# Scores of 28 tiles as two 64-row matmuls into two PSUM banks, in an attention and max-FFN kernel

## The chip, the cores and the metric

The kernel runs on one core of one Trainium2 chip. The metric is device microseconds of one execution. Nothing runs on the other cores.

## The reference, cut to what matters

Two parts follow each other. The first is attention over 8 batches and 8 heads (head size 64) with 512 local and 32 global positions. A local query sees the 32 global keys and the local keys at most 32 positions away; a global query sees everything. The second is a feed-forward over the 4352 resulting rows of 512: three products, their maximum, and a product back.

```python
s_ll = scale * np.matmul(q_l, k_l.transpose(0, 1, 3, 2))
mask = np.abs(pos[:, None] - pos[None, :]) <= window          # window = 32
s_l = np.concatenate([scale * np.matmul(q_l, k_g.transpose(0, 1, 3, 2)), np.where(mask, s_ll, -1e9)], axis=-1)
out_l = np.matmul(sm(s_l), np.concatenate([v_g, v_l], axis=2))
...
h = np.maximum(np.maximum(x @ w1, x @ w2), x @ w3)            # 512 -> 768
return (h @ w_out).astype(np.float32)                          # 768 -> 512
```

Only the scores `q k^T` of the local queries are touched by the change; the numbers that come out are the same.

## The kernel before, in words

**Tiles.** A tile is 128 query positions of a pair of heads (j = 0 and 1). Each of the 32 pairs (4 pairs per batch) has four tiles t = 0 to 3, so there are 128 tiles; t = 0 and 3 have 192 keys, t = 1 and 2 have 224 (`WIN`). One turn of the main loop (line 567) treats tile i, and calls in this order: `trans` of tile i+1 (its probabilities are turned by TensorE, lines 362 and 363), some matmuls of the feed-forward of the batch before (`fill`, lines 441 and 462), `scores` of tile i+3 (lines 335 or 339), more feed-forward, `pv` of tile i (probabilities times values, lines 401 or 409), and the work on weights and loads. The first 16 tiles go in an order of their own (`SEQ`), with tile halves of the keys (`kh`). `glob` (lines 285 and 289) makes the scores of the global queries, `late` (lines 504, 513, 519) those of the first batch, which were left out at the start.

**Split and unsplit.** Most products are made of operands that were split into a high and a low part and go through TensorE as `F32R`. For the first tiles the split would cost VectorE, ScalarE and GpSimd time that they need for the weights, so the scores of tiles 0 to 27 (`NATK`) and the products with values of tiles 0 to 25 (`NAT`) take plain `F32` operands. These are the unsplit tiles. A plain matmul shows in the trace as two passes, each with a weight load of its own.

**The scores of an unsplit tile.** The key tile holds the 64 dimensions of head 0 on partitions 0 to 63 and those of head 1 on partitions 64 to 127. The stationary operand is 128x128 for each head: the host writes head 0's queries over 64 rows of zeros, and for head 1 zeros over the queries (`qz`, lines 643 to 647). Each matmul thus takes all 128 rows, and both heads' results lie in one PSUM bank, `ps[:, 0:224]` and `ps[:, 224:448]`.

**What follows a score.** VectorE takes mask, scale and row minimum in one instruction per head (line 342), ScalarE the exponential (line 344), then come the sum's reciprocal and the multiplication (lines 347, 348 and the helper `times`, lines 121, 123, 125).

**PSUM.** `pm` has three banks for the feed-forward. `psS` has two one-bank buffers (name `S` in the trace): scores, the turned global probabilities (line 381), the global scores and those of `late`. `psT` has one bank (`T`). `psO` has one buffer of two banks (`O`): `pv` and the last product of `late`. `pv` copies its result out into `xr` (helper `copy`, lines 113 and 115).

**Weights.** The 24 weight blocks arrive in double precision and are taken apart by ScalarE (line 175), VectorE (176, 177, 180, 181) and a split (103, 113, 115), one or two blocks per tile (`WS`).

**Order.** Helpers choose an engine by a running cost sum (`least`). Within that the tile framework places every instruction on its engine by a planned time and adds the semaphores; the order of the source is not the order of the engines, and where an instruction may start decides where it is put. DMAs go out on SP's queue in its order.

Of the kernel before, what the change touches and what calls it, by code (L numbers as in the profile page):

```python
# [9 lines left out]
F32 = mybir.dt.float32  # L10
# [8 lines left out]
B, H, SL, SG, D = 8, 8, 512, 32, 64  # L19
DM, DF = 512, 768  # L20
NP = H // 2
# [4 lines left out]
NATK = range(0, 28)  # L26
# [24 lines left out]
def f32(ap):  # L51
    return ap.bitcast(F32)


def body(ctx, tc, kin, qin, vin, min_, win, out):
    nc = tc.nc
    act, dve, pool, pe = nc.scalar, nc.vector, nc.gpsimd, nc.tensor

    const = ctx.enter_context(tc.tile_pool(name="const", bufs=1))
    att = ctx.enter_context(tc.tile_pool(name="att", bufs=2))  # L60
# [3 lines left out]
    psS = ctx.enter_context(tc.tile_pool(name="psS", bufs=2, space=PSUM))  # L64
    psT = ctx.enter_context(tc.tile_pool(name="psT", bufs=1, space=PSUM))
    psO = ctx.enter_context(tc.tile_pool(name="psO", bufs=1, space=PSUM))
# [15 lines left out]
    def spend(es, ns):  # L82
        for e in es:
            load[e] += ns
# [122 lines left out]
    NAT = 26  # L207
    EARLY = 16
    SEQ = [4 * p + t for h in range(2) for p in range(NP) for t in (2 * h, 2 * h + 1)] + list(range(16, NS))
    kraw, kst, qraw, qs, vraw, vs, xr, sc, pg, pts = [{} for _ in range(10)]  # L210
# [32 lines left out]
    def load_q(s):  # L243
        if s < NS:
            if s in NATK:
                e = s < EARLY and SEQ.index(s) % 2
                qraw[s] = att.tile([128, 256], F32, name="qn", tag="qraw" if e else "qs")
            else:
                qraw[s] = att.tile([128, 256], F32, name="qraw")
            nc.sync.dma_start(out=qraw[s], in_=qin[s])  # L250

    def split_q(s):
        if s < NS and s not in NATK:
# [60 lines left out]
    def scores(sl):  # L314
        if sl >= NS:
            return
        p, t = divmod(sl, 4)
        c0, n = WIN[t]
        ps = psS.tile([128, 512], F32, name="S")
        if sl < EARLY:  # L320
            s = sc[sl] = early[:, SEQ.index(sl) % 4]
        else:
            s = att.tile([128, 2, 224], F32, name="s")
            sc[sl] = prob[sl % 2]
        nm = small.tile([128, 2], F32, name="nm")
        z = small.tile([128, 2], F32, name="z")
        ph = [ps[:, 0:224], ps[:, 224:448]]
        if sl < EARLY:
            keys, c0 = khalf[p][0], c0 - khalf[p][1]
        elif sl in NATK:  # L330
            keys = kraw[p]
        for j in range(2):
            if sl in NATK:

                pe.matmul(ph[j][:, 0:n], lhsT=qraw[sl][:, 128 * j:128 * j + 128], rhs=keys[:, c0:c0 + n],  # L335
                          start=True, stop=True)
                continue
            for a in range(2):
                pe.matmul(ph[j][:, 0:n], lhsT=qs[sl][:, a, 128 * j:128 * j + 128],  # L339
                          rhs=kst[p][:, j, c0:c0 + n], start=(a == 0), stop=(a == 1))  # L340
        for j in range(2):
            dve.tensor_tensor_reduce(out=s[:, j, 0:n], in0=ph[j][:, 0:n], in1=mask[:, (1, 0, 1, 0)[t], 32 * (t == 0):32 * (t == 0) + n],  # L342
                                     scale=-0.125, scalar=3.0e38, op0=ALU.add, op1=ALU.min, accum_out=nm[:, j:j + 1])
            act.activation(out=s[:, j, 0:n], in_=s[:, j, 0:n], func=AF.Exp, bias=nm[:, j:j + 1], scale=-1.0,  # L344
                           accum_out=z[:, j:j + 1])
        for j in range(2):
            dve.tensor_scalar(out=z[:, j:j + 1], in0=z[:, j:j + 1], scalar1=1e-9, scalar2=None, op0=ALU.add)  # L347
            dve.reciprocal(out=z[:, j:j + 1], in_=z[:, j:j + 1])
            times(s[:, j, 0:n], s[:, j, 0:n], z[:, j:j + 1])
        if sl >= EARLY:  # L350
            nc.sync.dma_start(out=f32(sc[sl])[:, :, 0:n], in_=s[:, :, 0:n])
        spend("d", 2 * (n * 1.04 + 75) + 150)
        spend("a", 2 * (n * 0.833 + 278))
# [37 lines left out]
    def pv(sl):  # L391
        p, t = divmod(sl, 4)
        pt = pts.pop(sl)
        o = psO.tile([128, 2, 512], F32, name="O")
        if t == 0:
            xr[p] = xp.tile([128, 4, 160], F32, name="xr")
        if sl < NAT:

            for c, j in ((0, 0), (0, 1), (1, 0), (1, 1)):
                n = 160 if sl >= EARLY and c < GCH[t][2] else 128  # L400
                pe.matmul(o[64 * j:64 * j + 64, 0, 0:n], lhsT=vraw[sl][:, 2 * j + c], rhs=pt[:, j, c, 0:n], start=(c == 0), stop=(c == 1))  # L401
            n = 160 if sl >= EARLY else 128
            copy(xr[p][:, t, 0:n], o[:, 0, 0:n], True)
        else:

            for j in range(2):
                for c in range(2):
                    n = 160 if c < GCH[t][2] else 128
                    pe.matmul(o[:, j, 0:320].rearrange("p (a q) -> p a q", a=2)[:, :, 0:n],  # L409
                              lhsT=vs[sl][:, 2 * j + c].rearrange("p a d -> p (a d)"),  # L410
                              rhs=pt[:, j, c, :, 0:n], start=(c == 0), stop=(c == 1))
            lo = att.tile([64, 2, 160], F32, name="lox", bufs=1)
            copy(lo, o[64:128, :, 0:160], True)
            spend("d", 460 + 2 * 320)
            dve.tensor_tensor(out=lo, in0=o[0:64, :, 160:320], in1=lo, op=ALU.add)
            for j in range(2):
                dve.tensor_tensor(out=xr[p][64 * j:64 * j + 64, t], in0=o[0:64, j, 0:160], in1=lo[:, j], op=ALU.add)  # L417
        if t == 3 and sl >= EARLY:
            dve.tensor_reduce(out=xg[:, p % NP, p // NP], in_=xr[p][:, :, 128:160].rearrange("p t g -> p g t"),
                              axis=AX.X, op=ALU.add)  # L420
# [75 lines left out]
    def late(p):  # L496
        k, v = side[:, 0:640], side[:, 640:1664].rearrange("p (t x) -> p t x", t=4)
        nc.sync.dma_start(out=k, in_=kin[p])
        nc.sync.dma_start(out=v, in_=vin[4 * p:4 * p + 4].rearrange("t p x -> p t x"))
        yield  # L500
        s, nm, z = side[0:64, 0:NG], small.tile([64, 2], F32, name="nmg"), small.tile([64, 2], F32, name="zg")
        for i, (c0, n) in enumerate(SEG):
            ps = psS.tile([128, 512], F32, name="S")
            pe.matmul(ps[0:64, 0:n], lhsT=k[:, KW:KW + 2 * SG], rhs=k[:, c0:c0 + n], start=True, stop=True)
            dve.tensor_tensor_reduce(out=s[:, 384 * i:384 * i + n], in0=ps[0:64, 0:n], in1=zero[0:64].to_broadcast([64, n]),
                                     scale=-0.125, scalar=3.0e38, op0=ALU.add, op1=ALU.min, accum_out=nm[:, i:i + 1])
            spend("d", n * 1.04 + 75)
        yield
        soft(s, nm, z)
        yield  # L510
        g = psS.tile([128, 512], F32, name="S")
        for x, (t, c, c0) in enumerate(PARTS):
            pe.transpose(g[:, 64 * x:64 * x + 64], side[0:64, c0:c0 + 128], one[0:64, 0:64])
        gt = att.tile([128, 6, 64], F32, name="gt", tag="lox", bufs=1)
        dve.tensor_tensor(out=gt, in0=g[:, 0:384].rearrange("p (x g) -> p x g", g=64), in1=cover.to_broadcast([128, 6, 64]), op=ALU.mult)
        o = psO.tile([128, 2, 512], F32, name="O")
        for x, (t, c, _) in enumerate(PARTS):
            for j in range(2):
                pe.matmul(o[64 * j:64 * j + 64, 0, 0:SG], lhsT=v[:, t, 64 * (2 * j + c):64 * (2 * j + c) + 64],
                          rhs=gt[:, x, SG * j:SG * j + SG], start=(x == 0), stop=(x == 5))  # L520
        copy(xg[:, p, 0], o[:, 0, 0:SG], True)
        yield
# [15 lines left out]
    def next_scores(last):  # L538
        while ahead[0] <= last:
            i = ahead[0]  # L540
            scores(tile_at(i))
            split_q(tile_at(i + 1))
            load_q(tile_at(i + 4 if i < 12 else i + 3))
            if i < 16 and i % 2 and i // 2 + 3 < 8:
                load_half(i // 2 + 3)
            ahead[0] += 1
# [20 lines left out]
    for i, sl in enumerate(SEQ):  # L567
# [52 lines left out]
        elif i % 16 >= 12:  # L620
            q = b * NP + i % 16 - 12
# [9 lines left out]
def _pack(q_l, k_l, v_l, q_g, k_g, v_g):  # L631
# [8 lines left out]
    g = np.concatenate([ga, gb], axis=3).transpose(0, 1, 3, 4, 2, 5).reshape(B, NP, 128, 2 * SG)  # L640
    k = np.ascontiguousarray(np.concatenate([k, g], axis=3)).reshape(B * NP, 128, KW + 2 * SG)
    q = q_l.reshape(B, NP, 2, 4, 128, D).transpose(0, 1, 3, 5, 2, 4).reshape(B * NP * 4, D, 256)
    q2 = q.reshape(B * NP * 4, D, 2, 128)
    z = np.zeros_like(q2[:, :, 0])
    qz = np.concatenate([np.concatenate([q2[:, :, 0], z], axis=2), np.concatenate([z, q2[:, :, 1]], axis=2)], axis=1)
    q = np.concatenate([q, q], axis=1)
    q[NATK.start:NATK.stop] = qz[NATK.start:NATK.stop]
    vt = [v_l[:, :, 32 * u:32 * u + 32] for u in range(16)] + [v_g]
    zero = np.zeros_like(v_g)
    v = np.concatenate([x for r in VROWS for x in [vt[u] for u in r] + [zero] * (4 - len(r))], axis=2)  # L650
# [1 line left out]
    q, v = np.ascontiguousarray(q), np.ascontiguousarray(v)  # L652
# [34 lines left out]
```

## Time and profile before

| | us |
|---|---|
| median of 3 runs (lowest, highest) | 829.01 (828.31, 830.57) |
| the profiled execution | 830.49 |
| span of its instructions | 828.7 |
| PE (TensorE matmul) busy | 803.0 (97%) |
| PEld (TensorE weight load) busy | 683.8 (83%) |
| DVE (VectorE) busy | 614.8 (74%) |
| ACT (ScalarE) busy | 510.2 (62%) |
| POOL (GpSimd) busy | 459.3 (55%) |

The span begins with the first instruction and ends with the last; 1.8 us of the profiled execution lie around it. Busy shares are means over stages: the unsplit scores run only in the first 130 us of the span, and what a change there is worth is read from the stretches of that time. The end of a matmul is modelled in the trace, so that pipelined matmuls overlap in it; what a pass really occupies is the distance between two starts.

### The profile page before, as it was taken

How to read it: one execution, taken by the hardware profiler on the slowest of the kernel's cores; microseconds unless marked ns; L12 is line 12 of the kernel's file. 1: busy time of each engine (PE TensorE's matmuls, PEld its weight loads, DVE VectorE, ACT ScalarE, POOL GpSimd, SP SyncE). 2: the span in 40 equal slices, each digit the busy share in tenths (PEclk: the TensorE clock that was granted, in tenths of full speed). 3: DMA queues.
4: the chain of work that ended last, by engine and by line, in shares of the span. 5: the costliest groups of instructions: out<-in, count | busy, mean ns of one | idle time of the engine just before them, and what ended most of it. 6: DMA issues, size and time to landing. Idle time of an engine off the chain costs nothing.

```text
span 828.7 us, 16580 instructions
## 1 busy us (share of the span) xinstructions
PE 803.0 (97%) x4772; PEld 683.8 (83%) x4772; DVE 614.8 (74%) x2192; ACT 510.2 (62%) x1416; POOL 459.3 (55%) x623
## 2 busy tenths in 40 slices
PE   6788999999999999999999999999999999999997
PEld 5577888888888888888888888888888888888896
DVE  6999997878887888888887888788887888412111
ACT  5888786666666666666766667676666666311111
POOL 3223355756676667767675676866776665311211
PEclk9989999999999999999999999999999999999999
DMA  8956555533335333443335333443335332100001
GB/s 295 314 178 224 169 152 149 165 116 99 116 108 152 112 97 104 131 136 94 99 104 170 112 98 97 127 139 98 97 96 165 110 100 63 60 13 1 25 27 26
DMA packets 97466, 98.15 MB, mean 118 GB/s; under 512 B 19296, under 2 KB 85856, under 8 KB 97376
## 3 DMA queue, kind: packets, MB, share of 16 engines
q1 hardware_dynamic: 97232, 96.87, 38.0%
q8 instruction: 38, 0.62, 0.3%
q14 instruction: 52, 0.43, 0.2%
q10 hardware_dynamic: 144, 0.23, 0.1%
HBM read 60.39 MB, written 8.91 MB: 84 GB/s over the span
## 4 chain that ended last, share of the span: by engine, by line
PE 80%; DVE 5%; DMA 4%; issue 3%; ACT 3%; POOL 3%; SPq 1%; POOLq 0%; ACTq 0%; DVEq 0%
PE pm L441 45%; PE pm L462 16%; PE O L409 6%; PE S L339 5%; PE T L362 2%; PE T L363 2%; DMA prob<-s 2%; PE S L289 1%; PE S L335 1%; POOL h L103 1%; PE O L401 1%; DMA vraw<-v_in 1%; ACT s L344 1%; PE S L381 1%; DMA raw<-w_in 1%
## 5 line engine op out<-in xcount | busy, mean ns | idle before, releaser
L441 PE MATMUL pm<-xs,w 128*128 128x512 f32 (+1 forms) x2160 | 487.3, 366 | 1.3 <-ACT m L115 0.9
L441 PEld LDWEIGHTS pm<-xs,w 128*128 128x128 f32 x2160 | 354.3, 190 | 52.7 <-issue 4.2
L462 PE MATMUL pm<-w,h 128*128 128x512 f32 x612 | 157.5, 397 | 2.3 <-POOL h L103 2.1
L103 POOL TENSOR_TENSOR h<-m,h 128x512 fp32r<-128x512 f32 (+1 forms) x59 | 70.3, 1192 | 108.5 <-ACT h L115 107.9
L462 PEld LDWEIGHTS pm<-w,h 128*128 128x128 f32 x612 | 109.0, 188 | 23.0 <-POOL h L103 4.4
L450 DVE TENSOR_TENSOR m<-pm,m 128x512 f32<-128x512 f32 (+1 forms) x120 | 72.8, 607 | 66.3 <-PE pm L441 65.6
L103 POOL TENSOR_TENSOR qs<-qraw,qs 128x256 fp32r<-128x256 f32 x100 | 76.7, 767 | 70.4 <-issue 34.8
L344 ACT ACTIVATE s<-s,nm 128x192 f32<-128x192 f32 (+1 forms) x224 | 103.3, 462 | 19.6 <-DVE nm L342 14.1
L125 POOL TENSOR_SCALAR s<-s,z 128x224 f32<-128x224 f32 (+1 forms) x192 | 83.9, 444 | 36.1 <-ACT lox L115 20.4
L342 DVE CUSTOM_DVE_ANT_0 s<-S,mask 128x192 f32<-128x192 f32 (+1 forms) x224 | 74.5, 369 | 15.2 <-PE S L339 7.0
L103 DVE TENSOR_TENSOR pt<-T,pt 128x512 fp32r<-128x512 f32 x102 | 70.4, 690 | 19.4 <-ACT pt L115 18.2
L103 POOL TENSOR_TENSOR vs<-vraw,vs 128x256 fp32r<-128x256 f32 x102 | 75.6, 741 | 12.6 <-ACT vs L115 9.3
L409 PEld LDWEIGHTS O<-pt,vs 128*128 128x128 f32 x408 | 66.2, 188 | 9.9 <-issue 1.6
L409 PE MATMUL O<-pt,vs 128*128 128x320 f32 (+1 forms) x408 | 72.9, 300 | 1.4 <-DVE pt L103 1.4
L339 PEld LDWEIGHTS S<-kst,qs 128*128 128x128 f32 x400 | 59.5, 190 | 8.7 <-DVE nmg L293 0.2
L417 DVE TENSOR_TENSOR xr<-O,lox 64x160 f32<-64x160 f32 x204 | 64.4, 315 | 3.1
L103 POOL TENSOR_TENSOR kst<-kraw,kst 64x576 fp32r<-64x576 f32 x44 | 63.9, 1453 | 4.3 <-DMA prob<-s 1.0
L115 ACT CAST pt<-T 128x512 fp32r<-128x512 f32 x102 | 60.3, 591 | 9.5 <-PE T L363 7.1
L115 ACT CAST qs<-qraw 128x256 fp32r<-128x256 f32 x94 | 38.3, 407 | 44.0 <-PE S L339 28.8
L115 ACT CAST h<-m 128x512 fp32r<-128x512 f32 (+1 forms) x59 | 33.2, 562 | 51.7 <-DVE m L450 51.6
L339 PE MATMUL S<-kst,qs 128*128 128x192 f32 (+1 forms) x400 | 59.5, 270 | 0.0
L347 DVE TENSOR_SCALAR z<-z 128x1 f32<-128x1 f32 x256 | 37.5, 147 | 27.1 <-ACT s L344 17.9
(123 smaller groups left out, 1183.7 us busy)
## 6 DMA issues: line engine op xcount, KB each, us to landing
vraw<-v_in SPq DMA_DIRECT2D x122, 128.0 KB, 2.3
qraw<-q_in SPq DMA_DIRECT2D x100, 128.0 KB, 2.2
prob<-s SPq DMA_DIRECT2D x56, 224.0 KB, 2.5
raw<-w_in SPq DMA_DIRECT2D x24, 512.0 KB, 5.3
prob<-s SPq DMA_DIRECT2D x56, 192.0 KB, 2.3
out_dram<-o SPq DMA_DIRECT2D x32, 256.0 KB, 2.4
kraw<-k_in SPq DMA_DIRECT2D x25, 320.0 KB, 3.1
qn<-q_in SPq DMA_DIRECT2D x29, 128.0 KB, 3.6
```

The costliest lines, as they stand in the source:

```text
L103: (dve if least(c) == "d" else pool).tensor_tensor(out=out, in0=a, in1=b, op=ALU.subtract)
L115: act.copy(out=out, in_=a)
L125: pool.tensor_scalar(out=out, in0=a, scalar1=col, scalar2=1.0, op0=ALU.mult, op1=ALU.mult)
L339: pe.matmul(ph[j][:, 0:n], lhsT=qs[sl][:, a, 128 * j:128 * j + 128], rhs=kst[p][:, j, c0:c0 + n], start=(a == 0), stop=(a == 1))
L342: dve.tensor_tensor_reduce(out=s[:, j, 0:n], in0=ph[j][:, 0:n], in1=mask[:, (1, 0, 1, 0)[t], 32 * (t == 0):32 * (t == 0) + n], scale=-0.12 ...
L344: act.activation(out=s[:, j, 0:n], in_=s[:, j, 0:n], func=AF.Exp, bias=nm[:, j:j + 1], scale=-1.0, accum_out=z[:, j:j + 1])
L347: dve.tensor_scalar(out=z[:, j:j + 1], in0=z[:, j:j + 1], scalar1=1e-9, scalar2=None, op0=ALU.add)
L409: pe.matmul(o[:, j, 0:320].rearrange("p (a q) -> p a q", a=2)[:, :, 0:n], lhsT=vs[sl][:, 2 * j + c].rearrange("p a d -> p (a d)"), rhs=pt[ ...
L417: dve.tensor_tensor(out=xr[p][64 * j:64 * j + 64, t], in0=o[0:64, j, 0:160], in1=lo[:, j], op=ALU.add)
L441: pe.matmul(ps[:, 0:n], lhsT=weight(3 * f + i, w)[:, 128 * k:128 * k + 128], rhs=xs[k][:, a, c0:c0 + n], start=(q == 0), stop=(q == 11))
L450: dve.tensor_tensor(out=m[:, 0:n], in0=ps[:, 0:n], in1=m[:, 0:n], op=ALU.max)
L462: pe.matmul(ps, lhsT=hh[f][:, a, 128 * t:128 * t + 128], rhs=weight(18 + f, w), start=(q == 0), stop=(q == 17))
```

## The change

Each head's scores of an unsplit tile become a matmul over its own 64 rows: head 0 on partitions 0 to 63, head 1 on partitions 64 to 127 of one 128x128 stationary tile without zeros. In the built program they have the tile size 64x128 and the tile positions (0, 0) and (64, 0); before they had 128x128. The two results go to two banks, so these scores take the two-bank buffer of `psO`. In exchange `pv` of tiles 0 to 25 and the last product of `late` take a bank of `psS`. The query load of an unsplit tile takes 128 of the 256 columns: 64 KB in pieces of 512 bytes where there were 128 KB in pieces of 1024 bytes; the number of pieces stays 128.

```diff
             if s in NATK:
                 e = s < EARLY and SEQ.index(s) % 2
-                qraw[s] = att.tile([128, 256], F32, name="qn", tag="qraw" if e else "qs")
+                qraw[s] = att.tile([128, 128], F32, name="qn", tag="qraw" if e else "qs")
+                nc.sync.dma_start(out=qraw[s], in_=qin[s, :, 0:128])
...
-        ps = psS.tile([128, 512], F32, name="S")
+        if sl in NATK:
+            ps = psO.tile([128, 2, 512], F32, name="O")
+            ph = [ps[:, 0], ps[:, 1]]
+        else:
+            ps = psS.tile([128, 512], F32, name="S")
+            ph = [ps[:, 0:224], ps[:, 224:448]]
...
-                pe.matmul(ph[j][:, 0:n], lhsT=qraw[sl][:, 128 * j:128 * j + 128], rhs=keys[:, c0:c0 + n],
+                pe.matmul(ph[j][:, 0:n], lhsT=qraw[sl][64 * j:64 * j + 64], rhs=keys[64 * j:64 * j + 64, c0:c0 + n],
                           start=True, stop=True)
...
-        o = psO.tile([128, 2, 512], F32, name="O")
+        o = psO.tile([128, 2, 512], F32, name="O") if sl >= NAT else psS.tile([128, 1, 512], F32, name="S")
...
-        o = psO.tile([128, 2, 512], F32, name="O")
+        o = psS.tile([128, 1, 512], F32, name="S")
...
-    qz = np.concatenate([np.concatenate([q2[:, :, 0], z], axis=2), np.concatenate([z, q2[:, :, 1]], axis=2)], axis=1)
+    qn = np.concatenate([q[:, :, 0:128], q[:, :, 128:256]], axis=1)
     q = np.concatenate([q, q], axis=1)
-    q[NATK.start:NATK.stop] = qz[NATK.start:NATK.stop]
+    q[NATK.start:NATK.stop, :, 0:128] = qn[NATK.start:NATK.stop]
```

The framework places instructions anew; from about row 340 of TensorE's 1800 on, past the last unsplit tile, the order is the same again. Three places follow; lines of the changed program are 5 higher here, so that 335 is 340, 342 is 347, 362 is 367, 401 is 406, 441 is 446 and 504 is 509.

The first is TensorE at the start of the program, before: `kh` and `qn` are the loaded keys and queries, `early` the probabilities.

```order
L335 MATMUL S<-kh,qn 128x192 x2
L335 MATMUL S<-kh,qn 128x224 x2
L335 MATMUL S<-kh,qn 128x192 x2
L335 MATMUL S<-kh,qn 128x224 x2
L362 MATMUL T<-one,early 128x128
L363 MATMUL T<-one,early 64x128
```

And now:

```order
L340 MATMUL O<-kh,qn 128x192 x2
L340 MATMUL O<-kh,qn 128x224 x2
L340 MATMUL O<-kh,qn 128x192 x2
L367 MATMUL T<-one,early 128x128
L368 MATMUL T<-one,early 64x128
L367 MATMUL T<-one,early 128x128
L368 MATMUL T<-one,early 64x128
L340 MATMUL O<-kh,qn 128x224 x2
```

The scores of the fourth tile moved behind the turning of the first.

The second is VectorE a little later, before: the line 342 rows with `early` are the minima of the third tile's second head and of the fourth tile, lines 176 and 177 the first weight block.

```order
L342 ISA early,nm<-S,mask 128x192
L342 ISA nm 128x1
L121 TENSOR_SCALAR early<-early,z 128x192
L131 CAST identr<-one 128x128
L348 RECIPROCAL z<-z 128x1
L347 TENSOR_SCALAR z<-z 128x1
L342 ISA early,nm<-S,mask 128x224
L342 ISA nm 128x1
L348 RECIPROCAL z<-z 128x1
L342 ISA early,nm<-S,mask 128x224
L342 ISA nm 128x1
L121 TENSOR_SCALAR early<-early,z 128x224
```

And now, from the same minimum on:

```order
L347 ISA early,nm<-O,mask 128x192
L347 ISA nm 128x1
L121 TENSOR_SCALAR early<-early,z 128x224
L352 TENSOR_SCALAR z<-z 128x1
L176 TENSOR_SCALAR spare<-spare 128x512
L353 RECIPROCAL z<-z 128x1
L352 TENSOR_SCALAR z<-z 128x1
L177 TENSOR_SCALAR spare<-spare 128x512
L353 RECIPROCAL z<-z 128x1
L347 ISA early,nm<-O,mask 128x224
L347 ISA nm 128x1
```

The fourth tile's minima moved behind the first two steps of the first weight block.

The third is TensorE among the feed-forward, around the scores of the 21st tile of the loop (`kn` are whole keys, `pm` the feed-forward, `side` the operand of `late`), before:

```order
L441 MATMUL pm<-xs,w_1145 128x256 x2
L335 MATMUL S<-kn,qn 128x192 x2
L401 MATMUL O<-pt,vraw 64x160 x4
L504 MATMUL S<-side 64x384
L362 MATMUL T<-identr,prob_93 128x128
L363 MATMUL T<-identr,prob_93 96x128
```

And now:

```order
L446 MATMUL pm<-xs,w_1145 128x256 x7
L406 MATMUL S<-pt,vraw 64x160 x4
L446 MATMUL pm<-xs,w_1145 128x256
L340 MATMUL O<-kn,qn 128x192 x2
L509 MATMUL S<-side 64x384
L509 MATMUL S<-side 64x160
L446 MATMUL pm<-xs,w_1145 128x256 x3
```

The scores stood next to the product with values and now stand by themselves between others; for one tile (the 25th in the loop, 128x192) the two heads are moreover apart:

```order
L340 MATMUL O<-kn,qn 128x192
L406 MATMUL S<-pt,vraw 64x160 x2
L406 MATMUL S<-pt,vraw 64x128 x2
L286 MATMUL S<-kn 64x384
L386 MATMUL S<-identr,probg_96 128x128
L367 MATMUL T<-identr,prob_93 128x128
L368 MATMUL T<-identr,prob_93 96x128
L367 MATMUL T<-identr,prob_93 128x128
L368 MATMUL T<-identr,prob_93 96x128
L340 MATMUL O<-kn,qn 128x192
```

Between the two heads lie ten other matmuls, where nothing lay between them before.

More of the change, by code (lines that the diff above doesn't have):

```diff
@@ L246, in load_q @@
                 e = s < EARLY and SEQ.index(s) % 2
-                qraw[s] = att.tile([128, 256], F32, name="qn", tag="qraw" if e else "qs")
+                qraw[s] = att.tile([128, 128], F32, name="qn", tag="qraw" if e else "qs")
+                nc.sync.dma_start(out=qraw[s], in_=qin[s, :, 0:128])
             else:
                 qraw[s] = att.tile([128, 256], F32, name="qraw")
-            nc.sync.dma_start(out=qraw[s], in_=qin[s])
+                nc.sync.dma_start(out=qraw[s], in_=qin[s])
     def split_q(s):
@@ L326, in scores @@
         z = small.tile([128, 2], F32, name="z")
-        ph = [ps[:, 0:224], ps[:, 224:448]]
         if sl < EARLY:
@@ L642, in _pack @@
     q = q_l.reshape(B, NP, 2, 4, 128, D).transpose(0, 1, 3, 5, 2, 4).reshape(B * NP * 4, D, 256)
-    q2 = q.reshape(B * NP * 4, D, 2, 128)
-    z = np.zeros_like(q2[:, :, 0])
-    qz = np.concatenate([np.concatenate([q2[:, :, 0], z], axis=2), np.concatenate([z, q2[:, :, 1]], axis=2)], axis=1)
+    qn = np.concatenate([q[:, :, 0:128], q[:, :, 128:256]], axis=1)
     q = np.concatenate([q, q], axis=1)
-    q[NATK.start:NATK.stop] = qz[NATK.start:NATK.stop]
+    q[NATK.start:NATK.stop, :, 0:128] = qn[NATK.start:NATK.stop]
     vt = [v_l[:, :, 32 * u:32 * u + 32] for u in range(16)] + [v_g]
```

## The prediction, as put on record before the result was known

> **What bounds the kernel now.** I read the page's shares first and then the same busy times by stretches, because the scores that change all run before 130 us. The columns are the length of the stretch, the busy times of the five engines with their instructions, the granted TensorE clock, the busy share of the DMA engines and what they moved.
>
> ```profile
> core 0: us, PE busy (x) PEld busy (x) DVE busy (x) ACT busy (x) POOL busy (x), PEclk, DMA share, GB/s
> 0.00:20.00 20.00, 12.79 (x76) 10.01 (x76) 12.13 (x62) 10.65 (x33) 7.25 (x24) 1.00 0.89 292
> 20.00:83.00 63.00, 54.29 (x389) 44.09 (x388) 60.96 (x201) 53.05 (x148) 17.68 (x17) 0.95 0.72 240
> 83.00:120.00 37.00, 37.00 (x295) 31.13 (x294) 34.84 (x127) 30.02 (x91) 14.85 (x12) 0.95 0.52 159
> 120.00:146.00 26.00, 23.62 (x212) 21.37 (x211) 19.70 (x85) 16.77 (x50) 14.49 (x20) 1.00 0.52 152
> 146.00:828.00 682.00, 675.25 (x3809) 577.25 (x3807) 487.18 (x1719) 399.71 (x1096) 405.03 (x551) 1.00 0.33 99
> ```
>
> The limit changes twice. Up to 20 us the loads lead (the DMA engines are 89% busy, nobody else over 64%). From 20 to 83 us VectorE is busy for 60.96 of 63 us, 97%, and TensorE for 86%. From 83 us on TensorE leads, busy for 100%, 91% and 99% of the last three stretches. So a TensorE saving counts in full only from 83 us on. The chain of work that ended last says the same (start, length, what):
>
> ```profile
> 4.56 6.07 DMA raw<-w_in
> 10.65 0.54 ACT spare L175
> ...
> 77.76 4.86 DMA prob<-s
> 82.67 0.28 PE T L362
> ...
> 99.71 0.76 PE S L335 x4
> ```
>
> It goes through the landing of the first weight block at 10.65 us, then over VectorE, and by a DMA of probabilities onto TensorE at 82.67 us, where the scores are links of it themselves.
>
> **What the new form saves.** TensorE's timeline shows a tile's scores among the feed-forward: start, length, line, tiles, shape, number of passes.
>
> ```profile
> 99.54 0.92 PE L335 MATMUL S<-kn,qn 128*128 128x224 f32 x4
> 100.42 1.48 PE L441 MATMUL pm<-xs,w 128*128 128x256 f32 x11
> 102.46 0.76 PE L401 MATMUL O<-pt,vraw 128*64 128x160 f32 x8
> ...
> 110.67 0.81 PE L335 MATMUL S<-kn,qn 128*128 128x192 f32 x4
> ```
>
> A pass shows with 0.33 to 0.35 us, but follows the one before by (0.92 - 0.35) / 3 = 0.19 us with 224 keys and (0.81 - 0.33) / 3 = 0.16 us with 192. The same division gives (1.48 - 0.28) / 10 = 0.12 us for a feed-forward matmul. If the two heads' passes go through the two halves of the array side by side, two of a tile's four pass times vanish: 0.38 us or 0.32 us. No row of this trace has two 64-row halves at once. The nearest is line 401, where two heads take 64 columns each: eight passes in 0.76 us, (0.76 - 0.30) / 7 = 0.07 us apart, though one pass of 160 columns by the rate of the 224 ones lasts 0.135 us. There two halves do run together, and I take it for the rows too.
>
> The Trainium skill (TensorEngine Tiling (Array Packing), Theoretical Speedup) allows up to twice the speed where the contraction is 64 or less.
>
> **What it costs.** The same neighbourhood holds the price of changing between the whole array and a half. I cut the timeline at single matmuls:
>
> ```profile
> 96.28 0.28 PE L441 MATMUL pm<-xs,w 128*128 128x256 f32 x1
> 96.49 0.36 PE L401 MATMUL O<-pt,vraw 128*64 128x160 f32 x2
> ...
> 96.92 0.28 PE L401 MATMUL O<-pt,vraw 128*64 128x128 f32 x2
> 97.13 0.39 PE L441 MATMUL pm<-xs,w 128*128 128x256 f32 x1
> 97.13 0.50 PE L441 MATMUL pm<-xs,w 128*128 128x256 f32 x2
> ...
> 101.74 0.28 PE L441 MATMUL pm<-xs,w 128*128 128x256 f32 x1
> 101.95 0.27 PE L513 MATMUL S<-one,side 64*128 64x64 f32 x1
> ```
>
> From the last feed-forward matmul to the first of line 401 are 0.21 us in place of 0.12: 0.09 us lost. The same 0.21 us stand ahead of line 513, whose operand has 64 rows, so rows cost what columns cost. On the way back the first matmul starts 0.21 us after a pass of about 0.11 us, 0.10 us lost, and the second at 97.13 + 0.50 - 0.28 = 97.35, 0.22 us later in place of 0.12: its weights were not loaded ahead. A change thus costs 0.09 us, and a further 0.10 us where the new form loads 128 columns of weights (for line 401's 64 columns 0.05).
>
> The Trainium skill (TensorEngine Tiling (Array Packing), Key Properties) says that changing the tiling mode drains TensorE; the 0.21 us agree. It names no price. By its speedup alone the scores' slots would halve, by that rule they must first earn the drains.
>
> So a tile that stands alone among feed-forward pays two changes of 0.09 and two loads of 0.10 = 0.38 us and saves 0.32 or 0.38: nothing, or 0.06 us lost. Only next to another half-array product does it gain. I count the changes along both orders, between whole-array work, 64-column products (401, 285, 504, 519) and 64-row ones (513 and now 340): 88 before, 125 now in all, and from the 20th tile of the loop on, where TensorE leads, 42 and 61. The 19 more are 8 into the whole array and 10 into rows (0.19 us each) and 1 into columns (0.14): 3.6 us. Of those nine tiles four have 192 keys and four 224 with the heads together, 4 x 0.32 + 4 x 0.38 = 2.8 us; the ninth has its heads apart and saves nothing. **Term: 3.6 - 2.8 = +0.8 us.** Were the load into rows as cheap as the 0.05 us of columns, it would be +0.3; were the two halves not together, +3.6.
>
> **The loads and the start.** Four query loads stand on SP's queue ahead of the first weight block, each 64 KB smaller. At the 292 GB/s of the first stretch 4 x 64 KB take 0.9 us; with the number of pieces unchanged the gain may also be none. I take the middle: the block lands **0.5 us** earlier, and ScalarE's line 175, the chain's next link, with it. Against this the fourth tile's minima move behind the block's first VectorE steps:
>
> ```profile
> 10.13 0.38 DVE L342 CUSTOM_DVE_ANT_0 early<-S,mask 128x224 f32<-128x224 f32 x1
> ...
> 12.30 0.42 DVE L176 TENSOR_SCALAR spare<-spare 128x512 f32<-128x512 f32 x1
> ...
> 16.68 0.27 PE L362 MATMUL T<-one,early 128*128 128x128 f32 x1
> ```
>
> They come some 2.5 us later, and that tile is turned only at 16.68 us, 6.5 us after its first minimum, with about 3 us of work between; so the 2.5 us are covered, and without that cover up to 1 us would come back. The matmul of the first tile ends earlier, but the next must now wait until VectorE has read it; I set these two against each other at nothing. **Term: -0.5 us**, bounds -0.9 and +1.0. In the later stretch a query load less ahead of the probabilities (64 KB at 240 GB/s, 0.3 us) is taken at nothing.
>
> **One buffer instead of two.** From 20 to 83 us the scores of a tile may start only once VectorE has read the tile before; until now, the one before that. The matmul's queue neighbours behind it on TensorE (turning, values, feed-forward) wait with it. This happens already:
>
> ```profile
> 42.01 1.59 PE L335 MATMUL S<-kh,qn 128*128 128x224 f32 x4 [1.37 <-DVE nm L342]
> ```
>
> For VectorE it matters only if the scores come too late for its own next minimum. The gap that it leaves between two tiles:
>
> ```profile
> 41.55 0.39 DVE L342 CUSTOM_DVE_ANT_0 early<-S,mask 128x224 f32<-128x224 f32 x1
> ...
> 45.34 0.34 DVE L342 CUSTOM_DVE_ANT_0 early<-S,mask 128x192 f32<-128x192 f32 x1
> ```
>
> From 41.94 to 45.34 us are 3.4 us of other VectorE work, and a tile's matmuls need 0.8 to 0.9 us (1.6 us at the low clock of that place). TensorE now has its scores one place later in its order, so it mostly finds the buffer free. **Term: 0**, the cover being those 3.4 us; if it goes, the time of a wait is lost to VectorE. Behind 83 us the minima follow their matmul at once and tiles are 4 to 6 us apart, so the buffer is free. The values' move to `psS` has one answer: twice the buffers for the product, one user for another in the ring, nothing.
>
> **Sum.** +0.8 - 0.5 = +0.3 us against the profiled execution's 830.5 us (span 828.7 and 1.8 around), 830.8. That execution lies 1.5 us over the median of the runs shown, 829.0, so the forecast for the median is 829.3 us. A measurement of this kernel tells some 0.3%, 2.5 us, from no change.
>
> **The rivals.** *The two heads run one after the other* (the change doesn't do what it says). Then the passes stay four and the changes are paid: +3.6 - 0.5 = +3.1, 832.1 us, slower. For it: no row shows two 64-row halves together, and the two results go to different banks only now. Against: line 401's pairs. Chance 0.12.
>
> *The single buffer starves VectorE.* Place: the minima of the 6th to the 19th tile. It decides once TensorE comes more than about 2 us late to a tile's scores (3.4 us of gap less the matmuls). Priced by the wait that stands above: three tiles of the fourteen losing 1.4 us each make 4.2, with the sum +4.5, 833.5 us, slower. For it: VectorE is 97% busy, so nothing lost comes back. Against: the gap. Chance 0.12.
>
> *Going into rows costs nothing*, because two loads into different halves overlap and the drain hides behind waits. Then the TensorE-led stretch gains 2.8 and the start 0.5: -3.3, 825.7 us, faster. For it: the drains that I read are next to columns or a turning, not to a 64-row product. Against: the 0.21 us ahead of line 513. Chance 0.15.
>
> *The whole halving counts.* By the rows above 28 tiles x 4 passes are 14 x 4 x (0.16 + 0.19) = 19.6 us, half of it 9.8: with the start -10.3, 818.7 us. It needs TensorE to lead before 83 us, which 97% of VectorE excludes nearly: 0.03. The Trainium skill's speedup (TensorEngine Tiling (Array Packing), Theoretical Speedup) is this rival; the trace shows it for columns and not for rows.
>
> **How the numbers follow.** The forecast keeps 0.58; its own range, by the bounds of the terms, is 827.9 to 831.3 us. Reaching to the first and third rival gives 825.5 to 832.8 us and leaves out the starved VectorE, the whole halving and little else, under 2 in 10. Faster by over 0.3%: 0.18 from the two rivals and 0.05 from new placements that remove a wait, 0.23. Slower: 0.24 and 0.03, 0.27. Within: 0.50.
>
> **What would show it.** Right: pairs of passes of line 340 starting within 0.02 us of each other, a gap of 0.21 us ahead of and 0.10 us behind them, the first weight block landing near 10.1 us, VectorE still 97% busy up to about 83 us and reaching the turning of the 17th tile within 1 us of 82.67. Wrong: line 340's passes 0.16 us apart throughout (first rival), waits of line 347 for line 340 between 20 and 83 us (second), no gaps around line 340 (third), or TensorE and VectorE both ending the early part several us sooner.

## The result, and the profile after

| us | before | after |
|---|---|---|
| median (lowest, highest, runs) | 828.66 (828.27, 830.57, 4) | 838.65 (837.60, 839.85, 4) |
| the profiled execution | 830.49 | 837.75 |
| its span | 828.7 | 836.0 |
| mean granted TensorE clock, all runs | 0.992 to 0.998 | 0.984 to 0.990 |

The kernel is slower: ratio 1.0116, interval 1.0093 to 1.0140, 10 us between the medians. The forecast was 829.3, the range ended at 832.8. (The clock range of before is that of 20 of its 21 runs beside the first experiments; the other had 0.990.)

The same stretches of the changed kernel as in the prediction, with the same columns:

```profile
core 0: us, PE busy (x) PEld busy (x) DVE busy (x) ACT busy (x) POOL busy (x), PEclk, DMA share, GB/s
0.00:20.00 20.00, 12.88 (x68) 7.26 (x68) 11.08 (x57) 9.80 (x29) 6.57 (x23) 1.00 0.88 283
20.00:83.00 63.00, 53.62 (x398) 40.68 (x397) 61.50 (x206) 53.94 (x151) 18.65 (x17) 0.95 0.69 219
83.00:120.00 37.00, 34.16 (x254) 25.64 (x252) 30.98 (x108) 25.77 (x76) 13.06 (x11) 0.91 0.50 150
...
146.00:835.00 689.00, 681.60 (x3847) 583.23 (x3846) 495.13 (x1743) 403.56 (x1108) 409.54 (x558) 1.00 0.33 98
```

Two places differ. In the first 20 us VectorE has 11.08 us of work done where it had 12.13. From 83 to 120 us TensorE, which was busy for all 37.00 us, is so for 34.16 and at a granted clock of 0.91 instead of 0.95. Behind 146 us there are 38 more matmuls, which had been done earlier before, and 3.3 us at half clock (153.3 to 156.6 us, granted clock 0.50) that the trace of before does not have; a wait of 1.4 us stands ahead of that place in both traces. The feed-forward matmuls of line 441 (now 446) say when the time is lost: the 181st starts at 80.87 us before and 80.48 after, the 277th at 110.31 and 107.95, but the 301st at 117.38 and 122.70, and the 2001st at 796.50 and 803.43. So the profiled execution is not behind up to 110 us (it gains 2.4 us, partly because before spends 83.3 to 86.6 us at 0.50) and then loses.

**The start.** TensorE's timeline before (start, length, line, tiles, shape, passes, idle time ahead of it and its releaser), first the scores of the first four tiles, then turnings:

```profile
4.51 4.94 PE L335 MATMUL S<-kh,qn 128*128 128x192 f32 x16 [4.51 <-DMA qn<-q_in]
9.28 0.27 PE L362 MATMUL T<-one,early 128*128 128x128 f32 x1
...
12.94 0.27 PE L363 MATMUL T<-one,early 128*96 128x128 f32 x1
13.36 0.66 PE L401 MATMUL O<-pt,vraw 128*64 128x128 f32 x8
```

And after:

```profile
4.51 1.01 PE L340 MATMUL O<-kh,qn 64*128 64x192 f32 x4 [4.51 <-DMA qn<-q_in]
6.26 1.12 PE L340 MATMUL O<-kh,qn 64*128 64x224 f32 x4 [0.74 <-DVE nm L347]
8.19 1.01 PE L340 MATMUL O<-kh,qn 64*128 64x192 f32 x4 [0.81 <-DVE nm L347]
...
10.55 1.12 PE L340 MATMUL O<-kh,qn 64*128 64x224 f32 x4
...
12.20 0.42 PE L368 MATMUL T<-one,early 128*96 128x128 f32 x1
...
12.97 1.12 PE L406 MATMUL S<-pt,vraw 128*64 128x128 f32 x8
...
17.09 0.27 PE L368 MATMUL T<-one,early 128*96 128x128 f32 x1
```

One run of 16 passes has become four pieces, the second and third of which wait 0.74 and 0.81 us for the minima of the tile before. And the same transpose takes 0.42 us at 12.20 where it took 0.27, the same eight passes of values 1.12 us where they took 0.66: TensorE runs at its low clock until about 16.7 us, before only until some time ahead of 9.28 (single passes place the change at 8.2). The clock column (1.00 for this stretch) doesn't show it, the lengths do.

**The stall at 110 us.** TensorE before: values, then the global scores (285) and, without a wait, the turned global probabilities (381).

```profile
107.68 0.71 PE L401 MATMUL O<-pt,vraw 128*64 128x160 f32 x8
108.22 0.81 PE L285 MATMUL S<-kn 128*64 128x384 f32 x2
...
109.54 0.22 PE L381 MATMUL S<-identr,probg 128*128 128x128 f32 x1
```

TensorE after, and VectorE at the same time:

```profile
109.03 0.71 PE L406 MATMUL S<-pt,vraw 128*64 128x160 f32 x8
109.57 0.81 PE L286 MATMUL S<-kn 128*64 128x384 f32 x2
112.32 0.37 PE L386 MATMUL S<-identr,probg 128*128 128x128 f32 x1 [1.94 <-DVE xr L113]
```

```profile
107.54 0.72 DVE L113 CAST kst<-kraw 64x576 fp32r<-64x576 f32 x1
...
108.63 1.87 DVE L103 TENSOR_TENSOR kst<-kraw,kst 64x576 fp32r<-64x576 f32 x1
110.53 1.38 DVE L177 TENSOR_SCALAR wct<-wct 128x512 int32<-128x512 int32 x1
...
111.95 0.31 DVE L113 COPY xr<-S 128x160 f32<-128x160 f32 x1
```

The values (line 406) end near 109.7 us, but VectorE has a key split (`kst`) and a weight step in its queue and copies them out only at 111.95. Their bank is now one of the ring of two, the global scores (286) hold the other, and the turning of the global probabilities (386) needs one: TensorE stands for 1.94 us. Then its clock falls:

```profile
108.00:112.30 4.30, 2.38 (x17) 1.35 (x16) 4.24 (x9) 1.53 (x6) 3.06 (x2) 1.00 0.75 222
112.30:119.10 6.80, 6.78 (x27) 4.69 (x28) 4.32 (x18) 3.52 (x10) 1.27 (x1) 0.50 0.36 109
```

6.8 us at 0.50 cost 3.4 us of TensorE's work. Between the 277th and the 301st feed-forward matmul are 14.75 us now, 7.07 before; of these 7.7 us more, wait and low clock make 5.3. The rest is not traced; what stands between those matmuls is not the same work.

### The profile page after: what moved, and what is told of

It is laid out like the page before. It is cut to its first block, busy times and chain, and to the rows that moved or that the text cites. A ratio compares the mean times of both kernels' runs of the same rounds, so it can differ in the third digit from the quotient of the medians.

```text
span 836.0 us, 16588 instructions
## 1 busy us (share of the span) xinstructions
PE 806.6 (96%) x4772; PEld 676.9 (81%) x4772; DVE 618.6 (74%) x2192; ACT 510.0 (61%) x1416; POOL 458.7 (55%) x623
## 4 chain that ended last, share of the span: by engine, by line
PE 83%; DVE 6%; DMA 3%; ACT 2%; issue 2%; POOL 2%; SPq 1%; POOLq 0%; DVEq 0%; ACTq 0%
PE pm L446 47%; PE pm L467 16%; PE O L414 6%; PE S L344 5%; PE T L367 2%; PE T L368 2%; DMA prob<-s 2%; PE S L290 1%; PE S L406 1%; PE O L340 1%; POOL h L103 1%; PE S L386 1%; ACT s L349 1%; DVE s L347 1%; DMA qn<-q_in 1%
## 5 line engine op out<-in xcount | busy, mean ns | idle before, releaser
L347 DVE CUSTOM_DVE_ANT_0 s<-S,mask 128x192 f32<-128x192 f32 (+1 forms) x200 | 66.6, 370 | 10.9 <-PE S L344 8.1
```

## The experiments

The kernel before ran beside each group on the same chip, with medians of 829.11, 829.55, 829.83, 829.24 and 829.47 us; the ratios are against these.

**First theory and rival.** Theory: the buffers cost, above all the ring of two (the stall). Rival: the 64-row form itself costs. The new buffers with the old 128 rows:

```diff
-  lhsT=qraw[sl][64*j:64*j+64], rhs=keys[64*j:64*j+64, c0:c0+n]
+  lhsT=qraw[sl][:, 128*j:128*j+128], rhs=keys[:, c0:c0+n]      # queries with zeros again
```

> The new buffers with the old matmuls: 128 rows with zeros and full query loads, but two banks of psO for the unsplit scores and psS for the values. Ring theory (the values' result in psS is copied out late by VectorE, the turned global probabilities need that buffer, TensorE stands still and its clock falls): at least 5 us over the kernel before, 834 to 838 us, with the same wait of the turning for the copy. Row theory (the 64-row form costs more than it saves): within 1.5 us of the kernel before, 827 to 830 us.

Measured: 834.91 us, ratio 1.0065 [1.0041, 1.0088]. More than half of the 10 us is there without any 64-row matmul. Its waits have the same stall, but no half clock follows it in the traced execution, which was the fastest of the four (832.46 us):

```profile
PE S L385 <- DVE xr L113: 1.9, 1, 1.9
```

The key split of the first split pair taken from VectorE, in the changed kernel:

```diff
+        if 4 * p == NATK.stop:      # copies by act.copy, subtractions by pool.tensor_tensor
```

> The changed kernel, with the split of the keys of the first split pair taken from VectorE (casts on ScalarE, subtractions on GpSimd), so that it no longer stands ahead of the copy out of psS. Ring theory: the wait of about 2 us and most of the 6.8 us at half clock behind it go, 832 to 835 us, some wait being left around 140 us. Row theory: no change, 837 to 840 us.

Measured: 833.01 us, 1.0050 [1.0032, 1.0068]: 5.6 us less than the changed kernel. The wait for the copy is 0.99 us there instead of 1.94, and no half clock follows it. The same copy given to ScalarE:

```diff
-            copy(xr[p][:, t, 0:n], o[:, 0, 0:n], True)
+            act.copy(out=xr[p][:, t, 0:n], in_=o[:, 0, 0:n])   # from the 17th tile on
```

> The changed kernel, with the copy of the values' result from tile 16 on always by ScalarE and never by VectorE. Ring theory: both waits of TensorE for that copy go (near 110 and near 141 us), 829 to 833 us. Row theory: no change, 837 to 840 us.

Measured: 833.62 us, 1.0052 [1.0028, 1.0075]; 5 us less, though a wait of 1.3 us for ScalarE's copy is left in its trace. The change for the first sixteen tiles only (`if sl < EARLY` at the buffers and the rows):

> The change for the first 16 tiles alone; tiles 16 to 27 keep 128 rows and psS, and their values psO. Ring theory: the turned global probabilities begin with tile 16, so nothing waits for a copy any more: 826.5 to 830.5 us. Row theory: 16 of the 28 tiles still pay, some 833 to 835 us.

Measured: 832.89 us, 1.0051 [1.0030, 1.0072]. So the stall is one cause, worth about 5 us in the changed kernel, but some 4 us are left without it, and the first sixteen tiles, which end before the stall, cost nearly 4 by themselves.

**What are the other 4 us?** A theory from the clocks: these kernels' runs have mean clocks of 0.990 to 0.993, before 0.995. TensorE would be too sparsely filled in the early part, and the clock fall more often. Two kernels made it denser (each of the unsplit scores issued twice, in the first sixteen tiles or in all), one made before sparser (scores of the first sixteen tiles from the upper halves of the numbers, as BF16, in one pass instead of two), and one freed the ring in another way (values of the unsplit tiles in a `pm` bank).

```diff
+                for _ in range(2):      # e5 on the first-sixteen kernel, e6 on the changed kernel
                     pe.matmul(ph[j][:, 0:n], ...)
```

> The change for the first 16 tiles alone, as in the run before, with each of their 64-row score matmuls issued twice into the same place, so that TensorE works about as long as with 128 rows. Clock theory (the half-length scores leave TensorE too idle in the first 60 us, and its clock is halved more often): the mean granted clock returns to 0.994 or more and the time to 828.5 to 830.5 us, though TensorE does more. Form theory (what those tiles lose comes from the mode changes and the single buffer): no gain, 832 to 836 us.

> The changed kernel with each 64-row score matmul of all 28 tiles issued twice. Clock theory: about 4 us of the 10 come back, 833.5 to 836 us, as with the new buffers and 128 rows; the wait for the copy out of psS stays. Form theory: no gain or worse, 838 to 841 us.

```diff
+                if sl < EARLY:          # on the kernel before
+                    q1, k1 = [x.bitcast(BF16).rearrange("p (n t) -> p n t", t=2)[:, :, 1] for x in (q1, k1)]
```

> The kernel before, buffers and 128 rows untouched, but the scores of the first 16 tiles take the upper 16 bits of their operands as BF16, so they are less exact, and one pass each in place of two longer ones. TensorE has less to do in the first 60 us, and nothing else changes. Clock theory: slower than the kernel before by 2 to 5 us, 831 to 834 us, with a mean clock of 0.992 or less. Otherwise: the same or a little faster, 826.5 to 829.5 us.

```diff
-        o = ... psS.tile([128, 1, 512], F32, name="S")
+        o = ... pm.tile([128, 1, 512], F32, name="pm")
```

> The changed kernel with the values' product of tiles 0 to 25 in the feed-forward's three banks in place of psS. Ring theory: nothing but scores of split tiles and turned probabilities waits on psS, the 4 us or so of the wait go, what is left is the clock's share: 832 to 834.5 us. If the wait for psS is not the cause: 837 to 840 us.

Measured: 834.69 (1.0065 [1.0047, 1.0084]), 842.40 (1.0169 [1.0139, 1.0199]), 829.89 (0.9998 [0.9986, 1.0010]) and 834.69 us (1.0055 [1.0036, 1.0073]). The theory falls as it stood: the denser kernels did get their clock back, to 0.999 and 0.995 in the mean of the runs, and were not faster for it (1.8 us over the first-sixteen kernel, 3.8 over the changed one); the sparser one kept its time. The fourth one has no stall at 110 us, but the feed-forward, with a bank less, begins at 36.3 us instead of 20.5, so it doesn't answer for the ring alone.

**Buffers or rows, early or late?** The first sixteen tiles with the new buffers and 128 rows; the tiles from the seventeenth on alone in the new form; these with the keys' split off VectorE; and the first sixteen with two score buffers (every other tile's heads in the two banks of `psS`, values in `pm`).

> Only the first sixteen tiles get the new buffers (scores in the one two-bank buffer, values in the ring of two), and their scores keep 128 rows with zeros. The kernel before stands near 829, the same change with 64 rows for these tiles at 832.9. If one score buffer instead of two is what costs there (a tile's scores wait for the previous minima), nothing is regained: 832 to 834. If the sparser 64-row passes cost, by letting the clock fall more often, it is back at 829 to 830.5, with a mean clock near 0.995 instead of 0.991.

> The first sixteen tiles stay as before the change; only the tiles from the seventeenth on take 64 rows per head, with their scores in the two-bank buffer and their values in the ring of two. If the two parts of the loss are apart, this keeps the late one alone: the whole 10 less the 3.8 of the first sixteen, so 834 to 836. If the late loss needs the early delay (a mishap of order), it is near 829 to 831.

> As the run with the late tiles only, and the splitting of the first split pair's keys is taken from VectorE and given to ScalarE and GpSimd, so that the values' result is copied out of the ring at once. If the late loss is the turning of the global probabilities standing behind that copy, this is back at 828 to 830.5. If the late loss comes from the 64-row form, it stays at 834 to 836.

> The change for the first sixteen tiles only, but with two score buffers: every other tile puts its two heads into the two banks of the ring instead of the two-bank buffer, and the values of these tiles go to the feed-forward banks. If the one score buffer is what costs in the first sixteen tiles, this is back at 828 to 830.5. If the 64-row form itself costs through the clock, it stays at 832 to 834 with a mean clock near 0.991. The values in the feed-forward banks may add up to 1 of their own.

Measured: 833.24 (1.0033 [1.0018, 1.0049]), 833.02 (1.0040 [1.0022, 1.0058]), 832.22 (1.0025 [1.0009, 1.0040]) and 832.71 us (1.0033 [1.0016, 1.0050]). The first says that the early loss is there with 128 rows too: the new buffers make it, not the rows. The late tiles alone cost 3.2 us, between the two times expected, and between 100 and 125 us of their trace no matmul waits over 0.3 us for the copy `xr`: there VectorE does the copy at 108.10 us and the subtraction of the key split after it, at 110.31. So the stall of 110 us does not come with the late buffers alone, and taking the keys away gains only 0.8 there. The last does not answer its question. With a `pm` bank gone, the feed-forward begins at 38 us and TensorE stays at the low clock; from 30 to 40 us the granted clock is:

```profile
30.00:40.00 10.00, 8.56 (x39) 5.27 (x40) 8.26 (x30) 9.06 (x27) 1.38 (x1) 0.50 0.63 199
```

**The start.** This left the first four tiles, whose rows stand above. One buffer for these four alone on the kernel before, with 128 rows (the values of three of them go to the ring with it); the new form for the fifth to the sixteenth alone; the whole change without the scores of the first four; the same with the keys' split off VectorE.

```diff
+NEW = [s for s in SEQ[:4]]                        # e13, queries with zeros
+NEW = [s for s in SEQ[4:EARLY]]                   # e14
+NEW = [s for s in NATK if s not in SEQ[:4]]       # e15, e16
-        if sl in NATK:
+        if sl in NEW:
             ps = psO.tile([128, 2, 512], F32, name="O")
```

> The kernel before, but the first four tiles put their scores, with 128 rows and zeros, into the one two-bank buffer (their values go to the ring, the fourth's to the two-bank buffer). If the start alone makes the early loss, with TensorE waiting for the minima of each of these tiles, this takes 832 to 833.5, as the run with all of the first sixteen so did, and the clock stays cold past 12 us. If the loss is spread over the sixteen tiles, it takes 829.5 to 830.5.

> The new form, 64 rows and one buffer, for the fifth to the sixteenth tile only; the first four and those from the seventeenth on stay as before. If the start alone makes the early loss, this is back at 829 to 830.5 or a little below. If the loss is spread over the tiles, it takes 831.5 to 833.

> The whole change except for the scores of the first four tiles, which keep 128 rows and the ring of two. If the start and the late wait are separate losses, this takes what the late tiles alone take, about 833. If the late loss in the changed kernel is as large as its 10 only because the start pushed VectorE's queue into it, 831 to 833 as well; if neither matters and the 64 rows cost in every tile, 836 or more.

> The whole change except for the scores of the first four tiles, and with the first split pair's keys taken from VectorE. Both waits that I hold responsible are gone. If they are the whole loss, this takes 828 to 830. If the 64-row form costs by itself, 832 or more.

Measured: 834.71 (1.0060 [1.0044, 1.0075]), 829.67 (1.0006 [0.9991, 1.0021]), 831.22 (1.0026 [1.0013, 1.0038]) and 831.72 us (1.0022 [1.0009, 1.0034]). So the early loss arises at these four: one buffer there alone makes 5.5 us, the new form at the next twelve nothing (with the values of all sixteen in the ring), and the whole change without the first four is 7.4 us faster than the changed kernel. The 5.5 us are more than the 3.4 us of the first-sixteen kernel with 128 rows, which has the same start. In the traces 3.1 and 2.5 us of them stand at the first feed-forward matmul (23.61 and 22.98 us, 20.48 before); a wait of 1.8 us at 141 us (line 292, for the minima `nmg`) is in the four-tile kernel alone; in the other that wait takes 0.6 us. The start is thus worth some 3.4 to 5.5 us. TensorE at the start of the first of them:

```profile
4.46 1.62 PE L342 MATMUL O<-kh,qn 128*128 128x192 f32 x4 [4.46 <-DMA qn<-q_in]
6.82 1.86 PE L342 MATMUL O<-kh,qn 128*128 128x224 f32 x4 [0.74 <-DVE nm L349]
9.49 1.65 PE L342 MATMUL O<-kh,qn 128*128 128x192 f32 x4 [0.80 <-DVE nm L349]
...
14.78 0.42 PE L370 MATMUL T<-one,early 128*96 128x128 f32 x1
```

and of the third, all but the first four new, where the run is whole and the clock rises at about 10.7 us:

```profile
4.66 5.89 PE L344 MATMUL S<-kh,qn 128*128 128x192 f32 x16 [4.66 <-DMA qn<-q_in]
10.34 0.42 PE L371 MATMUL T<-one,early 128*128 128x128 f32 x1
...
12.33 0.27 PE L372 MATMUL T<-one,early 128*96 128x128 f32 x1
```

VectorE gets 12.86 us of work done in the first 20 us of this kernel, 9.30 us in the one before it. And the stall at 110 us is all but gone, although the ring is the same. The framework has put VectorE's work in another order: the copy starts at 106.11 us, and the subtraction of the key split, which stood ahead of it in the changed kernel, at 115.73. So the stall takes the ring and this order together, and with the old start the order is another; that is why removing the start or the stall each regains half of the loss or more, and why taking the keys away on top regains nothing. The wait there, in the kernel with all but the first four:

```profile
PE S L513 <- DVE xr L116: 0.4, 1, 0.4
```

**The rest.** The same buffers with 128 rows everywhere (all but the first four), and the whole change with 64 rows everywhere but two score buffers at the start:

```diff
+        if sl in SEQ[1:4:2]:        # e18: second and fourth tile
+            ph = [psS.tile([128, 512], F32, name="S") for j in range(2)]
```

> The new buffers for all tiles but the first four, and every score keeps 128 rows with zeros. With 64 rows this took 831.22. If the remaining 2 us are the buffers' (one for the scores, a ring of two for the rest), this takes 831 to 832.5. If they are the 64-row form's, it takes 829 to 830.

> The changed kernel with 64 rows per head in every tile, but the second and the fourth tile put their two heads into the two banks of the ring, so that the first four tiles have two score buffers as before the change. If the waiting at the start is the cause, this takes 830.5 to 832.5, like the run that left the first four tiles in their old form. If it is the 64-row form at the start, it stays at 835 to 838.65.

Measured: 830.69 (1.0014 [1.0001, 1.0027]) and 834.62 us (1.0059 [1.0039, 1.0078]). The first puts the rest of about 2 us between the two: 1.2 for the buffers, 0.5 more for the rows, neither outside the other's interval. It also gives the price of one buffer at the start by itself: the buffers-only kernel differs from it by the scores of the first four tiles alone, with 128 rows in both, and takes 4.2 us more (834.91 to 830.69), its stall included. The second run tells most, and fits neither expectation. It regains 4.0 us by the second buffer, not 7, and its rows show why:

```profile
4.51 1.01 PE L342 MATMUL O<-kh,qn 64*128 64x192 f32 x4 [4.51 <-DMA qn<-q_in]
5.28 0.98 PE L342 MATMUL S<-kh,qn 64*128 64x224 f32 x4
6.38 1.01 PE L342 MATMUL O<-kh,qn 64*128 64x192 f32 x4
7.15 0.99 PE L342 MATMUL S<-kh,qn 64*128 64x224 f32 x4
...
12.84 0.42 PE L370 MATMUL T<-one,early 128*96 128x128 f32 x1
13.19 1.12 PE L408 MATMUL S<-pt,vraw 128*64 128x128 f32 x8
```

The waits are gone, but the faster form ends the run of scores at 8.1 us instead of 9.4, TensorE's work runs out at 9.3 us, and the clock stays low until about 17 us. From the first tile's values to the next tile's it then takes 3.0 us (13.19 to 16.23) where it took 1.9 (13.36 to 15.24).

So the 10 us, as far as the medians carry it: +2.0 from the fifth tile on; +3.4 when the first four take 64 rows with two buffers (834.62 - 831.22); +4.0 when these have one buffer (838.65 - 834.62), which holds the stall. They make 9.4 us, the kernel before having been 0.6 us slower in these groups, and each step is uncertain by 1 to 2 us. No version was faster than the kernel before.

What stays open: how much of the 3.4 us is the low clock alone. The sparser version of before also keeps it until past 16 us and loses nothing, but its scores have half the passes, and TensorE is busy for 10.44 of its first 20 us instead of 12.79. The 2 us from the fifth tile on aren't traced to a row either. No run changed VectorE's order and nothing else, so how much of the loss is the framework's new order and how much the buffers themselves isn't separated.

## Why the prediction was wrong, point by point

- **The halves run together: right.** Cut at single passes, two of them take 0.43 us and four 0.60, and the 0.21 us ahead of a change are there:

```profile
103.82 0.28 PE L446 MATMUL pm<-xs,w 128*128 128x256 f32 x1
104.03 0.43 PE L340 MATMUL O<-kn,qn 64*128 64x192 f32 x2
...
104.03 0.60 PE L340 MATMUL O<-kn,qn 64*128 64x192 f32 x4
```

  The third pass adds the 0.16 us, the second and the fourth 0.01. The Trainium skill (TensorEngine Tiling (Array Packing), Theoretical Speedup) allows up to twice the speed where a dimension is 64 or less; here two pairs stand 0.16 us apart, where four single passes of 192 keys stood 0.16 us apart each before.
- **Changes against saved passes, +0.8 us: not contradicted, but not shown either.** 64 rows against 128 with the same buffers and the same start: 831.22 to 830.69, +0.5, with intervals that overlap.
- **The first weight block 0.5 us earlier: right in kind.** Its load ends at 9.78 us instead of 10.63, and the chain reaches the turning of the seventeenth tile at 82.56 us where it was 82.62:

```profile
4.51 5.27 DMA raw<-w_in
...
77.67 4.89 DMA prob<-s
```

  The mark "within 1 us of 82.67" thus held, and hid that gain and loss of the start had cancelled in this execution.
- **The fourth tile's minima: right.** They come 1.75 us later (11.88 us instead of 10.13), and the tile is turned at 16.96 us instead of 16.68: covered, as said.
- **The range: it doesn't follow from its terms.** Their bounds (+0.3 for the changes; -0.9 and +1.0 for the start) give sums of -0.6 to +1.8, so 828.4 to 830.8 us about the median of 829.0, not 827.9 to 831.3. The measured time lies outside both.
- **"One buffer instead of two. Term: 0, the cover being those 3.4 us": wrong, the first step that failed.** The cover was read between 41.94 and 45.34 us and taken for all of the early part. In the first 10 us VectorE has hardly anything else queued (it stood idle 4.7 and 0.85 us ahead of its first minima even before), and each tile's scores wait for the minima of the one before, 0.74 and 0.81 us. Measured in place of 0: 3.4 to 5.5 us by itself with 128 rows. The second rival had the mechanism, but placed it at the 6th to 19th tile; the fifth to sixteenth cost nothing (829.67), and from 20 to 83 us TensorE waits for the minima no more than before (1.5 us, 1.4 before).
- **"One user for another in the ring, nothing": wrong, the second step.** The values used to leave `O`, for which only the next values waited. In `psS` the turning of the global probabilities waits for their copy, 1.94 us where that copy stands behind VectorE's key split. Worth about 5 us in the changed kernel, under 1 us in the kernels whose order puts the copy first.
- **No term for the clock: the omission behind both.** Each lost microsecond was priced at itself. The wait of 1.94 us was followed by 6.8 us at 0.50, and the broken run at the start by 8 us more at the low clock. The sum treated a saving where TensorE doesn't lead as worth nothing; the last kernel loses 3.4 us by it, and in its trace the saving cut short the burst that raised the clock before. That the low clock makes the 3.4 us is not shown.

## What to carry to other kernels

When a change takes a buffer from two to one, look for the cover at the first tiles apart: there little is queued that could hide a wait. When a result moves into a shared ring, follow its reader's queue: the next user waits for everything that stands ahead of that reader. A pause or a shorter burst on TensorE can cost more than its own length by the clock that follows it, though not in every execution. And where a planner sets the order of the engines, a change of buffers changes that order too: compare the queues of both programs at every new wait.

## What the runs showed of the hardware

The stretches at half clock in all these traces, but for those that reach to the end of the program, last 3.4, 6.8, 10.2 or 17.1 us, multiples of 3.4. One (112.3 us) began after a stand of only 1.94 us; in the 3.4 us ahead of it TensorE had still run for 1.5. The Trainium skill (TensorE: Matmul & The Clock Gate, Part 1) describes a free-running window of about 3.4 us, one idle window lowering the clock and one busy window raising it; the lengths agree, but here 1.94 us of idle time, not a whole window, was enough.

The same wait didn't always do it: 1.93 us in the buffers-only kernel and 1.8 us at 141 us in the four-tile kernel had no half clock behind them. Where it falls seems to decide. Lay a grid of 3.41 us through the moments at which a trace's clock changes, and take TensorE's busy time in each cell up to 170 us, over all 20 traces. Every fall came behind a cell with at most 62% (after, 108.87 to 112.28 us: 1.51 of 3.41), every rise behind one with at least 91%. The wait of the buffers-only kernel lies across two cells (to 110.48 us: 2.92 of 3.41; to 113.90: 1.98 of 3.42). This is no complete rule: cells of 51 to 62% went either way, and three with 99 or 100% left the clock low.

By the same grid the start can be read. Before has a full cell from 4.77 to 8.18 us, behind which the clock rises. With 64 rows and two buffers TensorE works from 4.51 to 9.31 us as well, but this run falls into two cells with 2.46 and 2.23 us, and the first full one ends at 17.32 us. A run of 4.8 us can hold a whole cell or miss it, so in this trace the late rise may be in part a matter of where the grid lay.

The time also follows the clock from run to run: the first-sixteen kernel took 831.05 to 833.25 us in its five runs with a mean clock of 0.994 to 0.996, 832.5 in one with 0.990, and 836.1 to 836.4 in the four with 0.986, the same program.
